# Attention and two MLPs in one kernel: five units of raw weight words under way, batch 1 loaded before unit 6, and the first w_out unit converted ahead of the softmax splits

## The chip, the cores and the metric

One core of one Trainium2 chip. The metric is the time of one launch in device microseconds, the median of several runs; lower is better. The engines are PE (TensorE, matmuls), DVE (VectorE), ACT (ScalarE), POOL (GpSimd) and SP (SyncE, which here issues nearly all the DMAs). Each works through its own queue in order and waits on semaphores of the others.

## The reference

All in float32. The attention has 8 batches, 8 heads, 576 rows of 64; `p` has 32 rows a head. `x` then has 4608 rows of 512, and each MLP has `w_in` of 512x2048 and `w_out` of 2048x512.

```python
p_packed = sm_attn(p, k, v)          # softmax(p k^T / 8) v
out = sm_attn(q, p_packed, p_packed)
x = out.transpose(0, 2, 1, 3).reshape(B * S, H * D)
h = x @ w_in1
x = (h * (1.0 / (1.0 + np.exp(-h)))) @ w_out1
h = x @ w_in2
out = (h * np.clip(h + 3.0, 0.0, 6.0) / 6.0) @ w_out2
```

## The kernel before

**Stages.** A prologue computes the attention of batch 0. Then come nine blocks of 512 tokens through MLP 1, and at the end MLP 2 over pairs of blocks. Block j runs sixteen hidden columns f of 128: hidden(f), called H0 to H15 here (line 860 on, 6 matmuls of 512 columns on PE for j = 0), then SiLU and the split of g into `gh` (ACT, line 889) and `gl` (DVE, line 890), and with a lag of two the projection of f - 2, called P0 to P15 (lines 897 to 899, 12 matmuls). In block 0 the attention of batch 1 stands between them: transposes of k and q (line 377), scores (line 417), softmax and the product with v.

**Splits.** Each factor of a float32 product is kept as a high part and a rest, and a product takes three matmuls: high by high, high by rest, rest by high. Hidden columns of block 0 multiply `fused` (w_in folded with the packed values, four groups g of four columns, made by `fuse`, lines 417, 611 and 617) with the weights of the softmax (`a2h`, `a2l`, lines 555 and 561).

**Raw words and units.** `w_in1` and `w_out1` arrive as raw 64-bit words and are turned into float32 on the chip. That goes in 16 units of 512 KB x 2: `in(g, c)` (two for each group g) and `out(k)` (the columns f = 2k and 2k + 1 of w_out), in the order in(0,0), in(0,1), out 0, in(1,0), in(1,1), out 1, out 2, in(2,0), in(2,1), out 3, out 4, in(3,0), in(3,1), out 5, out 6, out 7: units 0 to 15. A unit is loaded by `load_raw` on SP into a `raw` tile (`RAW = 3` of them), and converted by `conv_a` and `conv_b` (ACT, lines 148 and 154), `conv_shift` and `conv_sign` (DVE, lines 163 and 167) and `conv_add` (POOL, lines 177 and 179). A w_out unit then has `conv_hi` (two casts on ACT, line 192) and `conv_lo` (two subtractions on DVE, line 199), which give the weights of P(2k) (`wr`) and P(2k + 1) (`wo`); `keep` stores the odd ones in DRAM. `ct`, which conv_b writes, has two buffers, `cr` has four.

**Order.** Everything stands in the queues in the order in which the Python code runs; there is no scheduler behind it. `Feed.plan` puts each unit's steps at ticks: `STARTS` gives a unit's first tick, and the load of a later unit stands at its sixth. `LOADS` puts the loads of batch 1 (`load_p`, `load_tail`, `load_next`) at ticks too. In block 0, one tick is run for each 4.5 matmuls. Before block 0 the units 0 and 1 are written out by hand (`beginning`, `ending`), unit 2 and the rest go by ticks. `fill` runs matmuls on PE whose result is not used. In the prologue, part of the rows that the weights `wr` will take serve as `spare` room for q and v (`two_kb`).

Of the kernel before, what the change touches and what calls it, by code (L numbers as in the profile page):

```python
# [18 lines left out]
def tile_pack_attention_two_mlps(ctx: ExitStack, tc, q, k, v, p, w_in1, w_out1, w_in2, w_out2, out):  # L19
    nc = tc.nc  # L20
    B, H, S, D = q.shape
    NP = p.shape[2]
    NT, DM = out.shape
    DFF = w_in1.shape[1]
    P = 128
    T = 512
# [4 lines left out]
    NF = DFF // P  # L31
# [3 lines left out]
    RAW = 3  # L35
# [11 lines left out]
    wts = opened(first_left, "wts")  # L47
# [3 lines left out]
    cv = opened(first_block, "cv", side="right")  # L51
# [26 lines left out]
    early = [True]  # L78
    load_queue = [nc.sync]
    banks = [(ps_h, "h"), (ps_h, "h"), (ps_acc, "acc0"), (ps_acc, "acc1"), (ps_h, "h"), (ps_h, "h"), (ps_acc, "acc2")]  # L80
    spare = [(f, n) for f in range(0, NF, 2) for n in range(2)]
    shared = {}

    def bank():
# [10 lines left out]
    def two_kb():  # L95
        f, n = spare.pop()
        if f not in shared:
            shared[f] = wts.tile([P, 2, T], F32, tag=f"wr{f}", name="spare")
        return shared[f][:, n]


# [6 lines left out]
    made = {}  # L108
    raws = {}
    kept = []  # L110

    def half_w(f):
        if f % 2 == 0:
            return wts.tile([P, 2, DM], F32R, tag=f"wr{f}", name=f"wr{f}")
        return gp.tile([P, 2, DM], F32R, tag="wo", name="wo", bufs=WO)

    def load_raw(key):
        raw = cv.tile([P, 2, 2 * T], I32, tag="raw", name="raw", bufs=RAW)
        for i in range(2):
            if key[0] == "in":  # L120
                _, g, c = key
                src = w_in1.bitcast(I32)[(2 * c + i) * P:(2 * c + i + 1) * P, 2 * g * T:2 * (g + 1) * T]
            else:
                f = 2 * key[1] + i
                src = w_out1.bitcast(I32)[f * P:(f + 1) * P, :]
            nc.sync.dma_start(out=raw[:, i], in_=src)
        raws[key] = raw
# [399 lines left out]
    def sum2(lo, hi):  # L527
        g = (hi - lo) // NP
        st["s2", lo] = s = at.tile([P, (2 * S - T) // NP, 1], F32, tag="s2s", name="s2s", bufs=2)
        nc.vector.reduce_sum(out=s[:, 0:g, 0], in_=groups(lo, hi), axis=AX.X)  # L530

    def rec2(lo, hi):
        s = st["s2", lo][:, 0:(hi - lo) // NP]
        nc.vector.tensor_scalar_add(out=s, in0=s, scalar1=EPS)
        nc.vector.reciprocal(out=s, in_=s)

    def mul2(lo, hi, engine):
        g = (hi - lo) // NP
        engine.tensor_tensor(out=groups(lo, hi), in0=groups(lo, hi), in1=st.pop(("s2", lo))[:, 0:g].to_broadcast([P, g, NP]), op=ALU.mult)
# [801 lines left out]
    class Feed:  # L1341
# [6 lines left out]

        def load(self):
            if self.loaded < len(self.keys):  # L1350
                load_raw(self.keys[self.loaded])
                self.loaded += 1

        def plan(self):
            self.steps, self.ready = {}, set(self.keys[:2])
            for first, key in zip(STARTS, self.keys[2:]):
                todo = [(0, conv_a), (1, conv_b), (3, conv_shift), (4, conv_sign), (6, conv_add)]
                if key[0] == "out":
                    todo += [(9, conv_hi), (11, conv_lo)]
                todo += [(todo[-1][0], self.ready.add)]  # L1360
                for off, fn in todo:
                    self.steps.setdefault(first + off, []).append((off, lambda fn=fn, key=key: fn(key)))
                self.steps.setdefault(first + 6, []).append((20, lambda: self.load()))
                if key[0] == "out":
                    self.steps.setdefault(first + 15, []).append((21, keep))
            for first, fn in LOADS:
                self.steps.setdefault(first, []).append((30, fn))
            self.last = max(self.steps)
# [10 lines left out]
        def end(self):  # L1379
            while self.at <= self.last:  # L1380
                self.advance()

    FILL = (9, 10, 8, 20)
    STARTS = (-9, -6, -2, 1, 6, 9, 12, 15, 20, 24, 28, 31, 37, 42)
    LOADS = [(1, lambda: load_p(1)), (1, lambda: load_tail(1, "k"))]
    LOADS += [(2 + i, lambda i=i: load_next(i + 1)) for i in range(6)]
    LOADS += [(8, lambda: load_tail(1, "v")), (9, lambda: load_tail(1, "q"))]
    feed = Feed()
    feed.plan()
    feed.at = min(STARTS)  # L1390
# [21 lines left out]
        load_nat(0, "v", c)  # L1412
    load_tail(0, "v")
    load_tail(0, "q")
    feed.load()
    feed.load()
    feed.load()

    def beginning(key):
        conv_a(key)  # L1420
        conv_b(key)

    def ending(key):
# [73 lines left out]
    exp2(*SOFT2[1])  # L1497
    ending(unit[1])
    feed.load()
    fill(FILL[2])  # L1500
    to = fuse_products(0, 0)
    fill(FILL[3])
    turn_on(AF.Silu)
    feed.advance()
    feed.advance()
    made_ = fuse_high(0, 0, to)
    sum2(*SOFT2[0])
    rec2(*SOFT2[0])
    mul2(*SOFT2[0], nc.vector)
    sum2(*SOFT2[1])  # L1510
    rec2(*SOFT2[1])
    mul2(*SOFT2[1], nc.vector)
    turn_u(0, 0)
    high_u(0, 0, st["u", 0, 0])
    fuse_low(0, 0, to, made_)
    low_u(0, 0, st["u", 0, 0])
    turn_u(0, 1)
    high_u(0, 1, st["u", 0, 1])
    low_u(0, 1, st["u", 0, 1])
    while feed.at < 0:  # L1520
        feed.advance()
    early[0] = False
# [97 lines left out]
```

## Time and profile before

| | us |
|---|---|
| median of 3 runs (1492.5 to 1494.75) | 1492.56 |
| the profiled execution, its own time | 1489.72 |
| its span | 1487.9 |
| PE busy in the span | 1451.9 (98%) |
| DVE busy | 1008.4 (68%) |
| ACT busy | 725.0 (49%) |

All times below are of the profiled execution, counted from the start of its span; 1.82 us lie around the span. A row of a timeline has start, duration, engine, line, operation, output and inputs, and in brackets how long the engine had stood idle and which instruction released it. The duration of a matmul is modelled; what it costs is read from one start to the next.

### The profile page before, as it was taken

To read this page: it belongs to the slowest core of one execution; us is meant where nothing else is said; L and a number is where in the kernel's file an instruction comes from. 1 tells how busy PE (TensorE), PEld (TensorE's weight loads), DVE (VectorE), ACT (ScalarE), POOL (GpSimd) and SP (SyncE) were. 2 spreads that over 40 slices of the span, in tenths; PEclk is the share of its full clock that TensorE was granted. 3 is DMA by queue.
4 is the path that set the end of the run, shared out by engine and by line. 5 is a ranking of instruction groups with operands and counts; after the bars stand their busy time and mean duration, and the time that the engine had idled before them with its cause. 6 is when DMAs were issued, how large, how long until landed. Compare 5 with 4: busy or idle time off the path is not lost.

```text
span 1487.9 us, 21936 instructions
## 1 busy us (share of the span) xinstructions
PE 1451.9 (98%) x8002; PEld 1179.2 (79%) x8002; DVE 1008.4 (68%) x1555; ACT 725.0 (49%) x1107; POOL 179.9 (12%) x133
## 2 busy tenths in 40 slices
PE   7789999999999999999999999999999999999998
PEld 4557677777777676778888888888888889999998
DVE  5676555555656565645754769776977787878777
ACT  4584545555555555465553344343533443444443
POOL 1332111111112111132320000000000000000000
PEclk8899999999999999999999999999999999999999
DMA  7793686857585767489964676678667867998887
GB/s 239 199 290 91 202 243 172 205 164 169 159 205 155 200 153 209 121 224 250 279 195 155 193 245 199 190 227 262 203 194 226 243 210 213 293 309 252 273 272 227
DMA packets 391051, 316.58 MB, mean 213 GB/s; under 512 B 185120, under 2 KB 288032, under 8 KB 390432
## 3 DMA queue, kind: packets, MB, share of 16 engines
q1 hardware_dynamic: 389048, 314.72, 72.8%
q8 instruction: 64, 1.05, 0.3%
q10 hardware_dynamic: 1896, 0.46, 0.2%
q14 instruction: 43, 0.35, 0.1%
HBM read 257.43 MB, written 57.67 MB: 212 GB/s over the span
## 4 chain that ended last, share of the span: by engine, by line
PE 88%; ACT 4%; DVE 4%; DMA 2%; issue 1%; SPq 1%; POOL 0%; ACTq 0%; DVEq 0%; POOLq 0%
PE acc L897 8%; PE b L1161 8%; PE b L1163 8%; PE b L1162 8%; PE b L1256 8%; PE acc L898 8%; PE acc L899 8%; PE b L1258 8%; PE b L1259 8%; PE hps L870 4%; PE hps L872 4%; PE hps L871 4%; PE abank L417 3%; DMA nat<-in_v_dram 1%; PE abank L481 1%
## 5 line engine op out<-in xcount | busy, mean ns | idle before, releaser
L890 DVE TENSOR_TENSOR gl<-hps,gh 128x512 fp32r<-128x512 f32 x144 | 99.2, 689 | 200.1 <-ACT gh L889 199.9
L1161 PE MATMUL b<-xc,ws 128*128 128x512 f32 (+1 forms) x560 | 205.7, 367 | 0.7 <-ACT x L963 0.7
L1258 PE MATMUL b<-ro,ws 128*128 128x512 f32 (+2 forms) x564 | 206.2, 366 | 0.0
L1259 PE MATMUL b<-ro,ws 128*128 128x512 f32 (+2 forms) x564 | 206.2, 366 | 0.0
L1163 PE MATMUL b<-xc,ws 128*128 128x512 f32 (+1 forms) x560 | 205.6, 367 | 0.0
L1162 PE MATMUL b<-xc,ws 128*128 128x512 f32 (+1 forms) x560 | 205.6, 367 | 0.0
L1204 DVE TENSOR_TENSOR ro<-g,ro 128x1024 fp32r<-128x1024 f32 (+1 forms) x140 | 161.4, 1158 | 42.2 <-ACT ro L1199 41.8
L1199 ACT CAST ro<-g 128x1024 fp32r<-128x1024 f32 (+1 forms) x140 | 131.8, 965 | 94.0 <-DVE g L1192 34.6
L882 ACT ACTIVATE hps<-hps 128x512 f32<-128x512 f32 x144 | 84.0, 583 | 141.8 <-PE hps L872 141.4
L1256 PE MATMUL b<-ro,ws 128*128 128x512 f32 (+2 forms) x564 | 138.9, 367 | 0.3
L897 PE MATMUL acc<-gh,wr 128*128 128x512 f32 x288 | 117.2, 407 | 5.3 <-ACT gh L889 5.3
L1161 PEld LDWEIGHTS b<-xc,ws 128*128 128x128 f32 x560 | 105.1, 188 | 14.2 <-ACT x L963 1.1
L1259 PEld LDWEIGHTS b<-ro,ws 128*128 128x128 f32 x564 | 105.9, 188 | 13.1
L1258 PEld LDWEIGHTS b<-ro,ws 128*128 128x128 f32 x564 | 105.9, 188 | 13.1
L897 PE MATMUL acc<-gh,wo 128*128 128x512 f32 x288 | 114.3, 397 | 1.9 <-DMA wo<-w1o 1.9
L1162 PEld LDWEIGHTS b<-xc,ws 128*128 128x128 f32 x560 | 105.1, 188 | 13.2
L1163 PEld LDWEIGHTS b<-xc,ws 128*128 128x128 f32 x560 | 105.1, 188 | 13.1
L1256 PEld LDWEIGHTS b<-ro,ws 128*128 128x128 f32 x564 | 102.9, 188 | 15.0 <-DVE ro L1204 2.1
L898 PE MATMUL acc<-gl,wr 128*128 128x512 f32 x288 | 114.4, 397 | 0.2 <-DVE gl L890 0.2
L899 PE MATMUL acc<-gh,wr 128*128 128x512 f32 x288 | 113.9, 396 | 0.0
L899 PE MATMUL acc<-gh,wo 128*128 128x512 f32 x288 | 112.9, 392 | 0.0
L898 PE MATMUL acc<-gl,wo 128*128 128x512 f32 x288 | 112.9, 392 | 0.0
(176 smaller groups left out, 2636.0 us busy)
## 6 DMA issues: line engine op xcount, KB each, us to landing
ws<-w2in SPq DMA_DIRECT2D x280, 256.0 KB
ws<-w2out SPq DMA_DIRECT2D x280, 256.0 KB
wo<-w1o SPq DMA_DIRECT2D x64, 512.0 KB
x1d<-x SPq DMA_DIRECT2D x18, 512.0 KB
raw<-in_moe_w_in_dram SPq DMA_DIRECT2D x16, 512.0 KB
raw<-in_moe_w_out_dram SPq DMA_DIRECT2D x16, 512.0 KB
praw<-in_moe_w_in_dram SPq DMA_DIRECT2D x32, 256.0 KB
praw<-in_moe_w_out_dram SPq DMA_DIRECT2D x32, 256.0 KB
```

Of the source, the lines that this page charges most:

```text
L890: nc.vector.tensor_sub(out=gl, in0=g, in1=f32(gh))
L897: mm(acc[e], lhsT=w[:, 0, s], rhs=gh, start=first, stop=False)
L898: mm(acc[e], lhsT=w[:, 0, s], rhs=gl, start=False, stop=False)
L899: mm(acc[e], lhsT=w[:, 1, s], rhs=gh, start=False, stop=last)
L1161: mm(ps, lhsT=wh, rhs=xs[k][:, 0, c], start=first, stop=False, skip_group_check=True)
L1162: mm(ps, lhsT=wh, rhs=xs[k][:, 1, c], start=False, stop=False, skip_group_check=True)
L1163: mm(ps, lhsT=wl, rhs=xs[k][:, 0, c], start=False, stop=last, skip_group_check=True)
L1199: nc.scalar.copy(out=t[:, 0], in_=v)
L1204: nc.vector.tensor_sub(out=t[:, 1], in0=self.operand(s), in1=f32(t[:, 0]))
L1256: mm(to, lhsT=wh, rhs=x, start=False, stop=last, skip_group_check=True)
L1258: mm(to, lhsT=wh, rhs=x, start=first, stop=False, skip_group_check=True)
L1259: mm(to, lhsT=wl, rhs=x, start=False, stop=False, skip_group_check=True)
```

## The change

Five raw units are loaded at the start in place of three. The two more lie in rooms of the later weights `wr12` and `wr8` (`ROOM`), which `spare` tiles fill before; for that a `spare` tile and the weights of two even columns now share one tile of four parts (`pairs`). Units 8, 9 and 13 use those rooms again later. Batch 1's p, k and the first q are loaded in the prologue, between units 5 and 7, and no longer by ticks in block 0. Unit 2 (out 0) is written out by hand: its shift, sign and add stand ahead of the splits of the softmax weights, its casts before and after `low_u(0, 1)`. The sums, reciprocals and multiplications of the two softmax halves are paired. `STARTS` has one entry less, and from the fourth unit on its ticks are one to two earlier.

```diff
     def load_raw(key, room=None):
+        if room is None:
+            raw = cv.tile([P, 2, 2 * T], I32, tag="raw", name="raw", bufs=RAW)
+        else:
+            raw = wts.tile([P, 2, 2 * T], I32, tag=f"wr{room}", name="raw")
...
-            self.steps, self.ready = {}, set(self.keys[:2])
-            for first, key in zip(STARTS, self.keys[2:]):
+            self.steps, self.ready = {}, set(self.keys[:3])
+            for first, key in zip(STARTS, self.keys[3:]):
...
-                self.steps.setdefault(first + 6, []).append((20, lambda: self.load()))
+                if key != self.keys[9]:
+                    self.steps.setdefault(first + 6, []).append((20, lambda: self.load()))
...
+    ROOM = {3: 12, 4: 8, 8: 12, 9: 8, 13: 12}
-    STARTS = (-9, -6, -2, 1, 6, 9, 12, 15, 20, 24, 28, 31, 37, 42)
-    LOADS = [(1, lambda: load_p(1)), (1, lambda: load_tail(1, "k"))]
-    LOADS += [(2 + i, lambda i=i: load_next(i + 1)) for i in range(6)]
-    LOADS += [(8, lambda: load_tail(1, "v")), (9, lambda: load_tail(1, "q"))]
+    STARTS = (-6, -2, 1, 5, 8, 11, 14, 18, 22, 26, 29, 35, 40)
+    LOADS = [(6, keep), (8, lambda: load_tail(1, "v")), (9, lambda: load_tail(1, "q"))]
...
-    feed.load()
-    feed.load()
-    feed.load()
+    for _ in range(5):
+        feed.load()
...
     ending(unit[0])
     feed.load()
+    load_p(1)
+    load_tail(1, "k")
+    load_next(4)
...
     ending(unit[1])
     feed.load()
+    load_next(6)
...
-    feed.advance()
-    feed.advance()
+    beginning(unit[2])
     made_ = fuse_high(0, 0, to)
-    sum2(*SOFT2[0])
-    rec2(*SOFT2[0])
-    mul2(*SOFT2[0], nc.vector)
-    sum2(*SOFT2[1])
-    rec2(*SOFT2[1])
-    mul2(*SOFT2[1], nc.vector)
+    for i in range(2):
+        sum2(*SOFT2[i])
+    for i in range(2):
+        rec2(*SOFT2[i])
+    for i in range(2):
+        mul2(*SOFT2[i], nc.vector)
+    ending(unit[2])
+    feed.load()
...
     high_u(0, 1, st["u", 0, 1])
+    conv_hi(unit[2])
     low_u(0, 1, st["u", 0, 1])
+    conv_lo(unit[2])
```

On PE and on POOL no row moves. On ACT, from behind the last split of the prologue to the first SiLU of block 0, there stands before (`cr_467` is unit 2, `cr_502` and `cr_513` units 3 and 4, `cr_542` unit 5, `cr_609` unit 6, `hps_521` is H0, `kdg` the tail of batch 1's k):

```order
L148 ACTIVATE cr_502<-raw_408 128x1024
L154 ACTIVATE ct_505<-raw_408 128x1024
L148 ACTIVATE cr_513<-raw_424 128x1024
L154 ACTIVATE ct_515<-raw_424 128x1024
L192 CAST wr0_528<-cr_467 128x512
L192 CAST wo_530<-cr_467 128x512
L148 ACTIVATE cr_542<-raw_507 128x1024
L882 ACTIVATE hps_521<-hps_521 128x512
L889 CAST gh_545<-hps_521 128x512
```

and now (`cr_495` is unit 2, `cr_541`, `cr_547`, `cr_567` units 3, 4, 5):

```order
L201 CAST wr0_533<-cr_495 128x512
L201 CAST wo_535<-cr_495 128x512
L157 ACTIVATE cr_541<-raw_185 128x1024
L163 ACTIVATE ct_543<-raw_185 128x1024
L157 ACTIVATE cr_547<-raw_188 128x1024
L163 ACTIVATE ct_549<-raw_188 128x1024
L157 ACTIVATE cr_567<-raw_413 128x1024
L891 ACTIVATE hps_555<-hps_555 128x512
L898 CAST gh_570<-hps_555 128x512
```

The two casts of unit 2, before between units 4 and 5, now stand ahead of unit 3.

On DVE, from behind the sign step of unit 1 to the second split of the softmax weights, there stands before:

```order
L530 TENSOR_REDUCE s2s_477<-soft_100 128x16
L534 TENSOR_SCALAR s2s_477<-s2s_477 128x16
L535 RECIPROCAL s2s_477<-s2s_477 128x16
L539 TENSOR_TENSOR soft_100<-soft_100,s2s_477 128x512
L530 TENSOR_REDUCE s2s_482<-soft_100 128x20
L534 TENSOR_SCALAR s2s_482<-s2s_482 128x20
L535 RECIPROCAL s2s_482<-s2s_482 128x20
L539 TENSOR_TENSOR soft_100<-soft_100,s2s_482 128x640
L550 STREAM_TRANSPOSE abank_487<-soft_100 128x512
L617 TENSOR_TENSOR fused_472<-abank_435,fused_471 128x512
L617 TENSOR_TENSOR fused_475<-abank_436,fused_474 128x512
L561 TENSOR_TENSOR a2l_493<-abank_487,a2h_489 128x512
```

and now:

```order
L539 TENSOR_REDUCE s2s_505<-soft_100 128x16
L539 TENSOR_REDUCE s2s_507<-soft_100 128x20
L543 TENSOR_SCALAR s2s_505<-s2s_505 128x16
L544 RECIPROCAL s2s_505<-s2s_505 128x16
L543 TENSOR_SCALAR s2s_507<-s2s_507 128x20
L544 RECIPROCAL s2s_507<-s2s_507 128x20
L548 TENSOR_TENSOR soft_100<-soft_100,s2s_505 128x512
L548 TENSOR_TENSOR soft_100<-soft_100,s2s_507 128x640
L172 TENSOR_SCALAR cr_495<-cr_495 128x1024
L176 SCALAR_TENSOR_TENSOR cr_495<-raw_182,cr_495 128x1024
L559 STREAM_TRANSPOSE abank_521<-soft_100 128x512
L626 TENSOR_TENSOR fused_500<-abank_463,fused_499 128x512
```

The second sum has moved to the front, and the shift and the sign of unit 2 stand ahead of the first transpose (line 559). After that, DVE has before:

```order
L163 TENSOR_SCALAR cr_502<-cr_502 128x1024
L167 SCALAR_TENSOR_TENSOR cr_502<-raw_408,cr_502 128x1024
L163 TENSOR_SCALAR cr_513<-cr_513 128x1024
L890 TENSOR_TENSOR gl_546<-hps_521,gh_545 128x512
L199 TENSOR_TENSOR wr0_528<-cr_467,wr0_528 128x512
L199 TENSOR_TENSOR wo_530<-cr_467,wo_530 128x512
L167 SCALAR_TENSOR_TENSOR cr_513<-raw_424,cr_513 128x1024
L890 TENSOR_TENSOR gl_566<-hps_549,gh_565 128x512
L163 TENSOR_SCALAR cr_542<-cr_542 128x1024
```

and now:

```order
L208 TENSOR_TENSOR wr0_533<-cr_495,wr0_533 128x512
L208 TENSOR_TENSOR wo_535<-cr_495,wo_535 128x512
L172 TENSOR_SCALAR cr_541<-cr_541 128x1024
L176 SCALAR_TENSOR_TENSOR cr_541<-raw_185,cr_541 128x1024
L172 TENSOR_SCALAR cr_547<-cr_547 128x1024
L899 TENSOR_TENSOR gl_571<-hps_555,gh_570 128x512
L176 SCALAR_TENSOR_TENSOR cr_547<-raw_188,cr_547 128x1024
L899 TENSOR_TENSOR gl_586<-hps_574,gh_585 128x512
L172 TENSOR_SCALAR cr_567<-cr_567 128x1024
```

The two subtractions for `wr0` and `wo` no longer stand between `gl` of H0 and the sign step of unit 4.

On SP, from the first load of a raw unit on, there stands before:

```order
L126 DMA raw_177<-in_moe_w_in_dram 128x1024 x2
L126 DMA raw_180<-in_moe_w_in_dram 128x1024 x2
L126 DMA raw_183<-in_moe_w_out_dram 128x1024 x2
L126 DMA raw_408<-in_moe_w_in_dram 128x1024 x2
L126 DMA raw_424<-in_moe_w_in_dram 128x1024 x2
L126 DMA raw_507<-in_moe_w_out_dram 128x1024 x2
L126 DMA raw_525<-in_moe_w_out_dram 128x1024 x2
L324 DMA pn_536<-in_p_dram 128x1x64 x2
L330 DMA kt_539<-in_k_dram 64x8x64
L351 DMA nat_553<-in_k_dram 128x4x64 x2
L351 DMA nat_573<-in_k_dram 128x4x64 x2
L351 DMA nat_579<-in_k_dram 128x4x64 x2
```

and now:

```order
L135 DMA raw_176<-in_moe_w_in_dram 128x1024 x2
L135 DMA raw_179<-in_moe_w_in_dram 128x1024 x2
L135 DMA raw_182<-in_moe_w_out_dram 128x1024 x2
L135 DMA raw_185<-in_moe_w_in_dram 128x1024 x2
L135 DMA raw_188<-in_moe_w_in_dram 128x1024 x2
L135 DMA raw_413<-in_moe_w_out_dram 128x1024 x2
L333 DMA pn_416<-in_p_dram 128x1x64 x2
L339 DMA kt_419<-in_k_dram 64x8x64
L360 DMA nat_421<-in_k_dram 128x4x64 x2
L360 DMA nat_424<-in_k_dram 128x4x64 x2
L360 DMA nat_427<-in_k_dram 128x4x64 x2
L360 DMA nat_430<-in_k_dram 128x4x64 x2
```

Units 3 and 4 (`raw_185`, `raw_188`) now wait for the rooms of q and v, no longer for the raw tiles of units 0 and 1; unit 5 takes the tile of unit 0; and batch 1's p and k stand ahead of unit 6.

## Rows read from the trace of the kernel before

**Rows 1.** Busy time by stage; columns: stretch, length, PE, PEld, DVE, ACT, POOL, PEclk, DMA share, GB/s.
```profile
40.00:60.00 20.00, 14.95 (x70) 11.57 (x69) 16.55 (x19) 12.53 (x17) 8.45 (x4) 0.83 0.66 191
60.00:80.00 20.00, 16.63 (x79) 12.00 (x79) 10.04 (x16) 11.34 (x18) 7.01 (x4) 0.83 1.02 251
80.00:100.00 20.00, 16.51 (x100) 10.48 (x100) 18.02 (x25) 15.94 (x23) 8.10 (x5) 1.00 0.97 304
100.00:120.00 20.00, 17.68 (x151) 13.93 (x149) 9.66 (x17) 15.66 (x23) 6.93 (x3) 0.91 0.62 192
140.00:160.00 20.00, 19.48 (x111) 14.81 (x109) 15.72 (x26) 12.44 (x19) 1.04 (x1) 1.00 0.17 36
```

**Rows 2.** Timeline of PE: start, duration in us, instruction, idle before it and releaser.
```profile
51.33 0.79 PE L897 MATMUL acc<-gh,wr 128*128 128x512 f32 x1 [5.05 <-ACT gh L889]
...
53.25 0.63 PE L897 MATMUL acc<-gh,wr 128*128 128x512 f32 x1
...
53.68 0.63 PE L898 MATMUL acc<-gl,wr 128*128 128x512 f32 x1
...
66.65 0.79 PE L870 MATMUL hps<-a2h,fused 128*128 128x512 f32 x1 [3.37 <-ACT fused L611]
...
73.38 0.39 PE L899 MATMUL acc<-gh,wr 128*128 128x512 f32 x1
...
73.61 0.39 PE L870 MATMUL hps<-a2h,fused 128*128 128x512 f32 x1
...
83.73 1.09 PE L417 MATMUL abank<-T,pT 64*32 64x512 f32 x14 [1.87 <-ACT T L93]
...
95.59 0.50 PE L870 MATMUL hps<-a2h,fused 128*128 128x512 f32 x1 [0.71 <-ACT fused L611]
...
97.23 0.50 PE L872 MATMUL hps<-a2h,fused 128*128 128x512 f32 x1 [0.91 <-DVE fused L617]
...
110.29 0.63 PE L466 MATMUL abank<-ident,soft 128*64 128x128 f32 x2 [2.32 <-ACT T L93]
...
114.79 0.39 PE L870 MATMUL hps<-a2h,fused 128*128 128x512 f32 x1
...
164.38 0.47 PE L897 MATMUL acc<-gh,wo 128*128 128x512 f32 x1 [1.88 <-DMA wo<-w1o]
```

**Rows 3.** Timeline of ACT, same columns.
```profile
46.93 1.14 ACT L154 ACTIVATE ct<-raw 128x1024 int32<-128x1024 uint32 x1 [2.31 <-POOL cr L179]
...
50.70 0.58 ACT L889 CAST gh<-hps 128x512 fp32r<-128x512 f32 x1
...
59.78 0.37 ACT L93 COPY kdg<-abank 64x256 f32<-64x256 f32 x1 [4.17 <-DVE kdg L93]
...
66.02 1.07 ACT L611 CAST fused<-abank 128x512 fp32r<-128x512 f32 x2
...
73.82 1.12 ACT L148 ACTIVATE cr<-raw 128x1024 f32<-128x1024 f32 x1 [6.74 <-DMA raw<-in_moe_w_in_dram]
...
79.92 1.14 ACT L148 ACTIVATE cr<-raw 128x1024 f32<-128x1024 f32 x1 [1.81 <-DMA raw<-in_moe_w_out_dram]
```

**Rows 4.** Timeline of DVE and POOL, same columns.
```profile
32.79 1.91 DVE L534 TENSOR_SCALAR s2s<-s2s 128x16 f32<-128x16 f32 x1
...
42.11 0.68 DVE L163 TENSOR_SCALAR cr<-cr 128x1024 int32<-128x1024 int32 x1
...
53.12 1.22 DVE L167 SCALAR_TENSOR_TENSOR cr<-raw,cr 128x1024 int32<-128x1024 int32 x1
...
54.49 2.39 POOL L177 TENSOR_TENSOR wi<-cr,ct 128x1024 int32<-128x1024 int32 x1 [3.69 <-DVE cr L167]
...
54.86 2.57 DVE L163 TENSOR_SCALAR cr<-cr 128x1024 int32<-128x1024 int32 x1
```

**Rows 5.** Timeline of SP's queue, same columns.
```profile
27.18 5.85 SPq L126 DMA_DIRECT2D raw<-in_moe_w_in_dram  x4
...
70.87 7.90 SPq L126 DMA_DIRECT2D raw<-in_moe_w_out_dram  x4
```

More of the change, by code (lines that the diff above doesn't have):

```diff
@@ L80, in tile_pack_attention_two_mlps @@
     banks = [(ps_h, "h"), (ps_h, "h"), (ps_acc, "acc0"), (ps_acc, "acc1"), (ps_h, "h"), (ps_h, "h"), (ps_acc, "acc2")]
-    spare = [(f, n) for f in range(0, NF, 2) for n in range(2)]
+    PAIRED = NF // 2
+    spare = [(f, n) for f in range(PAIRED, NF, 4) for n in range(4)]
     shared = {}
@@ L97, in two_kb @@
         if f not in shared:
-            shared[f] = wts.tile([P, 2, T], F32, tag=f"wr{f}", name="spare")
+            shared[f] = wts.tile([P, 4, T], F32, tag=f"wr{f}", name="spare")
         return shared[f][:, n]
@@ L110, in tile_pack_attention_two_mlps, with load_raw @@
     kept = []
+    pairs = {}
     def half_w(f):
+        if f % 2 == 0 and f < PAIRED:
+            return wts.tile([P, 2, DM], F32R, tag=f"wr{f}", name=f"wr{f}")
         if f % 2 == 0:
-            return wts.tile([P, 2, DM], F32R, tag=f"wr{f}", name=f"wr{f}")
+            if f % 4 == 0:
+                pairs[f] = wts.tile([P, 2, 2, DM], F32R, tag=f"wr{f}", name=f"wr{f}")
+            return pairs[f // 4 * 4][:, f % 4 // 2]
         return gp.tile([P, 2, DM], F32R, tag="wo", name="wo", bufs=WO)
-    def load_raw(key):
-        raw = cv.tile([P, 2, 2 * T], I32, tag="raw", name="raw", bufs=RAW)
+    def load_raw(key, room=None):
+        if room is None:
+            raw = cv.tile([P, 2, 2 * T], I32, tag="raw", name="raw", bufs=RAW)
+        else:
+            raw = wts.tile([P, 2, 2 * T], I32, tag=f"wr{room}", name="raw")
         for i in range(2):
@@ L1350, in load @@
             if self.loaded < len(self.keys):
-                load_raw(self.keys[self.loaded])
+                load_raw(self.keys[self.loaded], ROOM.get(self.loaded))
                 self.loaded += 1
         def plan(self):
-            self.steps, self.ready = {}, set(self.keys[:2])
-            for first, key in zip(STARTS, self.keys[2:]):
+            self.steps, self.ready = {}, set(self.keys[:3])
+            for first, key in zip(STARTS, self.keys[3:]):
                 todo = [(0, conv_a), (1, conv_b), (3, conv_shift), (4, conv_sign), (6, conv_add)]
```

## The prediction

> **What bounds the kernel now.** PE is busy for 98% of the span, so time can only come from where it stands idle or runs slowly, and the change touches nothing behind block 0. The busy times by stage are read first: PE works 14.95, 16.63, 16.51 and 17.68 us of the four 20 us stretches from 40 to 120, 14.2 us short, and its granted clock averages 0.83, 0.83, 1.00 and 0.91 [rows 1]. Then PE's timeline: the gaps are 5.05 us ahead of P0, 3.37 ahead of H4, 1.87 ahead of batch 1's scores, 0.71 and 0.91 in H8, and 2.32 ahead of line 466, 14.23 in all [rows 2]. After the gaps of 5.05, 3.37 and 2.32 PE starts at half clock: two matmuls start 0.43 us apart at 53.25, and 0.23 at 73.38 [rows 2], which are the levels of 1.2 and 2.4 GHz. After 0.71, 0.91 and 1.87 the clock stays up. The releasers say who is late: ACT each time but one, which is DVE, so ACT's timeline comes third. It waits 2.31 us for POOL at 46.93, 4.17 for DVE at 59.78, and 6.74 and 1.81 for raw units to land at 73.82 and 79.92 [rows 3]. DVE and POOL come last, then SP: from 70.87 it needs 7.90 us to issue units 9 and 10 [rows 5].
>
> **The change part by part.** I follow the new order of each queue from 32 us on, with durations of before. On ACT a conversion pass takes 1.05 us from start to start, a cast or SiLU 0.5 to 0.6; on DVE a shift is 0.6 and a sign step 1.15 from start to start; an add on POOL is 2.4 [rows 3, 4].
>
> *A, the way to P0.* The scale step at 32.79 takes 1.91 us because it sits out POOL's add for unit 1 [rows 4]. The second sum, 0.8 us, now stands ahead of it, inside that wait: with its latency 0.95 saved. Shift and sign of unit 2 come in, 1.8 us. So the last split, which ends at 42.11 [rows 4], ends about 0.85 later; PE runs its unused matmuls until about 42 anyhow and loses nothing there, since it idles before P0. On ACT, from the last `a2h` cast (at 41.4 before, 42.25 now) to the end of H0's `gh` lie five passes, two casts, a SiLU and a cast, 7.5 us; before, the 2.31 us wait came on top, and `gh` started at 50.70 and ended at 51.28 [rows 3]. That wait was for unit 2's add. The add now starts behind the sign step at about 38.7 and is over at 41.1. So `gh` ends at 49.8, and P0 starts 1.5 us sooner. This gap is still some 3.5 us, P0 still starts at half clock, and I take nothing for it. **A: 1.45.**
>
> *B, the way to H4.* The sign step of unit 4 starts at 53.12, behind `gl` and two subtractions (1.2 us) for P0's weights; POOL's add follows at 54.49, and the shift at 54.86 sits it out and takes 2.57 us in place of 0.68 [rows 4]. With those subtractions done earlier the sign step starts at 50.45, the add at 51.7, and the shift ends at 54.65, 2.8 us sooner. Behind it the same five operations lead to the `kdg` copy on ACT, now 57.0 for 59.78. From there to the cast of `fused` at 66.02 [rows 3] were 6.24 us; one pass, 1.05, now stands ahead of `kdg`, inside ACT's wait. So the cast starts at 62.2 and H4 at 62.7 for 66.65. **A and B: 4.0.** PE would be there at 63.28 - 1.45 = 61.8, which leaves a gap of 0.9.
>
> *C, H4 and P2.* These 18 matmuls took 73.61 - 66.65 = 6.96 us [rows 2] for 18 x 0.23 = 4.14 at full clock. After a gap of 0.9 the clock should stay up, as after 0.71 and 0.91 before: 2.8 gained. But DVE now has the shift of unit 7 ahead of the subtractions for `wr2`, and it meets POOL's add of unit 6 (62.4 to 64.8, or a microsecond earlier); `wr2` is ready at 66.0 where P2's third matmul would start at 64.8: 1.3 lost, and 0.25 for the low half of `fused`. **C: 1.25**, from 2.3 to -1.55 if the clock falls anyway.
>
> *D, batch 1's scores.* The 1.87 us hang on a `T` copy of ACT behind a pass that waited 1.81 us for a unit in DRAM. Units 8 and 9 are now issued behind the sign steps of units 3 and 4, at about 47 and 52, and needed after 63; SP has nothing blocked ahead of them. The copy ends at 73, PE arrives at 75. **D: 1.87.** Units 3 and 4, issued from 27.18 on before [rows 5], now wait only for the rooms of q and v, which the prologue has read by then, and stand in the queue behind units 0 to 2, so they hold up neither; batch 1's p and k then fill SP until about 37, and unit 7 lands before 50, wanted at 57. I take nothing for these loads: the work that hides them is the softmax of batch 0 and the conversion of units 0 to 4. Without that cover they would cost what a late unit cost before, the 1.81 us at 79.92 [rows 3].
>
> *E, H8.* The gaps were 0.71 + 0.91. DVE has one sign step more ahead of the split of `fused`, and I come to 0.6 + 1.45. **E: -0.4**, from 0 to -1.5.
>
> *F, line 466.* It waited 2.32 us for an ACT copy; it now waits for DVE's `gl` of H9, which I put at 100.6, with PE arriving at 100.35. **F: 2.05**, at least 0.8 if ACT is a microsecond late.
>
> *G.* Line 466 and the 12 matmuls of P8, 114.79 - 110.29 = 4.5 us [rows 2], need 3.05 with no gap ahead. **G: 1.45**, or 0.
>
> Sum 1.45 + 2.55 + 1.25 + 1.87 - 0.4 + 2.05 + 1.45 = 10.2. The profiled execution took 1489.72 (span 1487.9), 2.84 below the median; it would take 1479.5. From the median of 1492.56: **1482.4 us**.
>
> **A rule against C and G.** The rows show half clock after gaps of 2.32 us and more, and none after 1.87 and less. The Trainium skill ("TensorE: Matmul & The Clock Gate", Part 1) says that the throttled state is the default, that activity releases it, and that the number of slow matmuls varies from run to run of one kernel. By that, a stretch of short waits like H4 to P2 may run slowly without one long gap. No run here shows it yet; the rival below has its price from rows.
>
> **The rivals.** *1. The clock stays low.* H4 to P2 and line 466 with P8 run slowly though their gaps are short. For it: PE stands still for some 2 us in H4 to P2 in pieces. Against: it did so in H8, 0.71 + 0.91, with no slow matmul. Price 2.8 + 1.45: gain 5.95, **1486.6**.
>
> *2. Nothing arrives at the end.* Block 1 opens with a 1.88 us wait for a load of `wo` at 164.38 [rows 2]. If that load came at a time of its own, what block 0 gains would be stood out there. Against: the DMA engines are busy for 0.17 of 140 to 160 [rows 1], so no backlog sets it, and the load is issued behind work of the same queues. That also covers a change that fails to pull the conversion ahead. Gain 0 to 3, **1491**.
>
> *3. Slower: ACT waits for POOL ahead of SiLU.* A `conv_b` needs a `ct` tile that POOL's add two units back sets free, and the SiLUs queue behind it. At 46.93 one such wait cost 2.31 us [rows 3]. With units further ahead in the queue than POOL, each of units 7 to 15 may pay it: nine times 2.31 is 20.8, against a gain of 10.2, **1503**. It decides from the fifth such wait on. Against: an add takes 2.4 us and I find the adds 6 us apart, with two waits of under 1.5 us, at units 8 and 9, where PE has slack.
>
> **How the numbers follow.** The forecast (gain 8 to 12) has 0.62, rival 1 0.2, rival 2 0.1, rival 3 0.05; 0.03 is left for a gain over 12. The range reaches from 1478.5 (14 us: all gaps and slow matmuls but A's) to 1489 (3.5: rival 1 with E and F at their lower ends), and holds the first two. 0.2% is 3 us, about what a measurement can tell from no change here. Faster: 0.62 + 0.2 + 0.03 and a little of rival 2, 0.86; the same 0.09; slower 0.05.
>
> **What would show it.** Right: P0 at about 49.8, with ACT in no wait for POOL ahead of it; the shift of unit 5 ending near 54.7; `kdg` near 57 and H4 near 62.7 after a gap of about 1 us at full clock; no ACT wait for a raw unit from 60 to 90; scores without a gap near 75; line 466 near 100.6. Wrong: matmuls 0.43 us apart behind 62; ACT rows waiting over 2 us for POOL; a gap of PE over 2 us anywhere from 60 to 115 (a step of the chain missed); or block 1's first wait much longer than 1.88.

## The result, and the profile after

The changed kernel takes **1480.21 us** (median; 1477.84 to 1482.2) against 1492.56 (1490.41 to 1494.75) for the kernel before, runs taken side by side: ratio 0.9917, 95% interval 0.9902 to 0.9931. The forecast was 1482.4, faster. The profiled execution took 1477.84 with a span of 1476.0, against 1489.72 and 1487.9. In the new file a helper's line has a number 9 higher.

Busy time by stage, the columns of [rows 1]:

```profile
40.00:60.00 20.00, 16.56 (x80) 12.68 (x79) 15.92 (x21) 16.20 (x23) 10.01 (x5) 0.91 0.90 284
60.00:80.00 20.00, 18.53 (x113) 12.12 (x112) 18.67 (x22) 16.30 (x23) 9.80 (x5) 1.00 1.02 307
80.00:100.00 20.00, 17.24 (x88) 12.90 (x87) 16.70 (x23) 16.34 (x24) 7.38 (x4) 0.91 0.71 206
100.00:120.00 20.00, 20.00 (x177) 14.60 (x176) 16.07 (x20) 12.81 (x21) 7.20 (x3) 1.00 0.43 83
```

PE's busy time rises in each stretch, and the last one is full. The low clock (0.91) stands in 80 to 100 now, where before it was 1.00.

PE's timeline, the rows that answer to [rows 2]:

```profile
49.78 0.49 PE L906 MATMUL acc<-gh,wr 128*128 128x512 f32 x1 [3.11 <-ACT gh L898]
...
51.78 0.63 PE L906 MATMUL acc<-gh,wr 128*128 128x512 f32 x1
52.21 0.63 PE L907 MATMUL acc<-gl,wr 128*128 128x512 f32 x1
...
62.91 0.50 PE L879 MATMUL hps<-a2h,fused 128*128 128x512 f32 x1 [1.31 <-ACT fused L620]
...
75.06 1.09 PE L426 MATMUL abank<-T,pT 64*32 64x512 f32 x16
...
76.44 0.50 PE L906 MATMUL acc<-gh,wr 128*128 128x512 f32 x1
...
89.44 0.80 PE L881 MATMUL hps<-a2h,fused 128*128 128x512 f32 x1 [2.03 <-DVE fused L626]
90.03 0.63 PE L879 MATMUL hps<-a2h,fused 128*128 128x512 f32 x1
90.46 0.63 PE L880 MATMUL hps<-a2l,fused 128*128 128x512 f32 x1
...
101.52 0.41 PE L475 MATMUL abank<-ident,soft 128*64 128x128 f32 x2
...
154.28 0.47 PE L906 MATMUL acc<-gh,wo 128*128 128x512 f32 x1 [1.96 <-DMA wo<-w1o]
154.59 0.40 PE L907 MATMUL acc<-gl,wo 128*128 128x512 f32 x1
154.82 0.40 PE L908 MATMUL acc<-gh,wo 128*128 128x512 f32 x1
```

H4's gap shrinks from 3.37 to 1.31 us. Batch 1's sixteen score matmuls stand in one row, and line 475 (466 before) shows no wait. One thing is worse: H8's third matmul waits 2.03 us for DVE, and the matmuls behind it start 0.43 us apart, which is 1.2 GHz.

ACT's `kdg` copy and the shift of unit 5 on DVE, for [rows 3] and [rows 4]:

```profile
57.02 0.37 ACT L94 COPY kdg<-abank 64x256 f32<-64x256 f32 x1 [1.70 <-DVE kdg L94]
...
62.26 1.08 ACT L620 CAST fused<-abank 128x512 fp32r<-128x512 f32 x2
```

```profile
50.37 1.22 DVE L176 SCALAR_TENSOR_TENSOR cr<-raw,cr 128x1024 int32<-128x1024 int32 x1
...
52.51 2.16 DVE L172 TENSOR_SCALAR cr<-cr 128x1024 int32<-128x1024 int32 x1
```

ACT waits for no raw unit from 40 to 120; its longest wait there for POOL is 1.26 us.

### The profile page after: what moved, and what is told of

Read it like the earlier page. It is cut to its first block, busy times and chain, and to the rows that moved or that the text cites. A ratio compares the mean times of both kernels' runs of the same rounds, so it can differ in the third digit from the quotient of the medians.

```text
span 1476.0 us, 21930 instructions
## 1 busy us (share of the span) xinstructions
PE 1447.3 (98%) x8002; PEld 1176.1 (80%) x8002; DVE 1013.0 (69%) x1555; ACT 725.6 (49%) x1107; POOL 179.9 (12%) x133
## 4 chain that ended last, share of the span: by engine, by line
PE 89%; DVE 4%; ACT 3%; DMA 2%; issue 1%; SPq 1%; POOL 0%; ACTq 0%; POOLq 0%; DVEq 0%
PE acc L906 8%; PE b L1170 8%; PE b L1171 8%; PE b L1172 8%; PE b L1265 8%; PE acc L907 8%; PE acc L908 8%; PE b L1268 8%; PE b L1267 8%; PE hps L879 5%; PE hps L881 4%; PE hps L880 4%; PE abank L426 3%; DVE cr L176 1%; PE abank L490 1%
```

## The experiments

For all kernels I read where PE's work starts, counted from the row of line 499 (508) near 20.8 us, since that row itself moves by up to 0.84 us from execution to execution. Times are medians; the runs of one kernel spread over 2 to 7 us, and the profiles show the clock falling at different waits. The kernel before was run again beside each group of experiments, with medians from 1490.73 to 1491.67, so times of different groups compare best by their ratios to it.

| kernel | us | P0 | H4 | P4 | H9 | 466/475 | H11 |
|---|---|---|---|---|---|---|---|
| before | 1492.56 | 30.56 | 45.88 | 64.33 | 80.25 | 89.52 | 94.02 |
| changed | 1480.21 | 28.71 | 41.84 | 55.37 | 73.67 | 80.45 | 83.44 |
| e1_order | 1489.07 | 28.71 | 44.22 | 62.93 | 78.42 | 87.72 | 92.29 |
| e2_loads | 1484.58 | 30.53 | 45.91 | 60.58 | 76.09 | 85.41 | 88.40 |
| e3_batch1_late | 1480.07 | 28.73 | 41.87 | 55.35 | 73.67 | 80.48 | 83.49 |
| e4_unit11_later | 1478.00 | 28.72 | 41.86 | 55.33 | 70.37 | 78.33 | 81.33 |
| e5_old_ticks | 1483.10 | 28.69 | 42.84 | 57.49 | 73.01 | 82.31 | 85.29 |
| e6_warm | 1477.48 | 28.83 | 41.88 | 56.43 | 72.19 | 79.62 | 82.64 |
| e7_late_casts | 1480.12 | 28.70 | 42.98 | 57.09 | 74.87 | 81.65 | 84.64 |
| e8_wo_early | 1475.29 | 28.71 | 42.26 | 55.73 | 70.80 | 78.74 | 81.73 |
| e9_both | 1476.17 | 28.73 | 42.31 | 55.82 | 70.86 | 78.48 | 81.46 |
| e10_three | 1482.68 | 29.19 | 43.27 | 56.76 | 75.10 | 82.04 | 85.02 |
| e11_after (changed, again) | 1479.57 | 28.71 | 41.86 | 55.36 | 72.12 | 79.59 | 82.57 |
| e12_three_late | 1487.73 | 28.71 | 45.71 | 61.19 | 80.92 | 87.72 | 90.72 |

### Order alone, loads alone, ticks alone

**Order alone** (the kernel before with unit 2 by hand and the paired softmax; old loads and ticks):

```diff
-    STARTS = (-9, -6, -2, 1, 6, 9, 12, 15, 20, 24, 28, 31, 37, 42)
+    STARTS = (-6, -2, 1, 6, 9, 12, 15, 20, 24, 28, 31, 37, 42)
...
+    beginning(unit[2])
...
+    ending(unit[2])
```

> The kernel before with the prologue's new order alone: unit 2 written out by hand as in the changed kernel, but three raw tiles, batch 1 loaded by ticks and the old ticks for units 3 on. Theory (A and B hang on the order, D on the loads): P0 starts near 49.8 in place of 51.33, H4 near 63 in place of 66.65, and ACT still waits for a raw unit of words ahead of unit 8 or 9, so batch 1's scores still stand behind a gap and most of the 4 us is given back there: 1487 to 1491. Rival 1 (the order makes nearly all of it): the gain of 10 to 12 us comes whole, 1480 to 1483, and no ACT wait for a raw unit over 1 us is left. Rival 2 (all of it is loads): P0 and H4 stand where they stood within 0.5 us and the time is that of before, 1492.5.

Measured 1489.07, ratio 0.9988 (0.9978 to 0.9997). P0 comes as early as in the changed kernel: term A belongs to the order. Also `kdg` comes at 56.91, where the changed kernel has it, but H4 only at 44.22, 2.4 us later than there (65.2 in the trace; I had expected 63). ACT stands idle for 1.31 us ahead of unit 7's first pass (the trace names a load of p as what ended it). And by the old ticks three conversion passes stand between `kdg` and the fused cast, where the changed kernel has two and the third ahead of `kdg`. PE still stalls at the scores. ACT and PE:

```profile
56.91 0.37 ACT L93 COPY kdg<-abank 64x256 f32<-64x256 f32 x1 [2.97 <-DVE kdg L93]
...
61.47 1.14 ACT L148 ACTIVATE cr<-raw 128x1024 f32<-128x1024 f32 x1 [1.31 <-DMA pn<-in_p_dram]
...
64.56 1.04 ACT L611 CAST fused<-abank 128x512 fp32r<-128x512 f32 x2
```

```profile
81.59 1.78 PE L417 MATMUL abank<-T,pT 64*32 64x512 f32 x14 [2.17 <-ACT T L93]
```

So B needs more than the order: the order frees the chain, and ACT must then neither wait for a load nor have the third pass behind `kdg`. The run without the new ticks (below) puts that pass at 1.0 us.

**Loads alone** (the changed kernel with the old order and old ticks):

```diff
-    STARTS = (-6, -2, 1, 5, 8, 11, 14, 18, 22, 26, 29, 35, 40)
+    STARTS = (-9, -6, -2, 1, 6, 9, 12, 15, 20, 24, 28, 31, 37, 42)
...
-    beginning(unit[2])
+    feed.advance()
+    feed.advance()
```

> The changed kernel with the prologue's old order and the old ticks: five raw units under way and batch 1 loaded early, and nothing else. Theory: P0 at 51.3 and H4 at 66.6 as before with the 5.05 and 3.37 us gaps, no ACT wait for a raw unit between 60 and 90, scores without a gap (2.9 us sooner), then line 466 (475 here) sooner by at most the same 2.9 plus its own gap: 1485 to 1489. Rival 1 (loads are hidden anyway, the order makes all of it): 1491 to 1493. Rival 2 (loads make all of it): 1480 to 1483.

Measured 1484.58, ratio 0.9961 (0.9948 to 0.9975), 0.4 under the theory's end. P0 and H4 stand where they stood, the scores have no gap, and ACT waits for no raw unit from 60 to 90:

```profile
80.03 1.09 PE L426 MATMUL abank<-T,pT 64*32 64x512 f32 x16
81.05 0.43 PE L439 MATMUL abank<-kdg,pT 128*32 128x128 f32 x8
81.41 0.50 PE L906 MATMUL acc<-gh,wr 128*128 128x512 f32 x1
```

From H5 to P4 it needs 8.57 us, as the changed kernel does; before, 11.49. The difference, 2.92, is term D measured by itself. Line 475 still waits 2.37 us here, as in order alone (2.35): neither part makes F.

**Ticks alone undone** (units 6 to 15; loads and order stay):

```diff
-    STARTS = (-6, -2, 1, 5, 8, 11, 14, 18, 22, 26, 29, 35, 40)
+    STARTS = (-6, -2, 1, 6, 9, 12, 15, 20, 24, 28, 31, 37, 42)
```

> The changed kernel with the old ticks for units 6 to 15 (each one to two later); loads and prologue order stay as changed. From the last prologue row on (PE's line 508 near 21 us), H4 stood at 41.84, H8 at 65.61, H9 at 73.67 and line 475 at 80.45 in the changed kernel. Theory (the ticks, and neither loads nor order, removed the wait ahead of line 475, and they made H8's): H4 at 41.8, H9 near 70.4 with no gap over 1 us in H8, then a gap of 2.4 us ahead of line 475 for an ACT copy, line 475 near 79.7 and P8 behind it slow or not: 1479 to 1481. Rival (loads and order removed the wait of line 475): line 475 near 77.2 without a gap, 1476 to 1477.5.

Measured 1483.1, ratio 0.9951 (0.9937 to 0.9964). H8 loses its long gap, and the wait ahead of line 475 is back: the ticks made both. In the profiled executions the two cancel: from P4 to line 475 it takes 25.19 us before, 25.08 in the changed kernel and 24.82 here. PE:

```profile
63.91 0.50 PE L879 MATMUL hps<-a2h,fused 128*128 128x512 f32 x1 [2.36 <-ACT fused L620]
...
65.45 0.63 PE L881 MATMUL hps<-a2h,fused 128*128 128x512 f32 x1
65.88 0.63 PE L906 MATMUL acc<-gh,wr 128*128 128x512 f32 x1
...
103.38 0.41 PE L475 MATMUL abank<-ident,soft 128*64 128x128 f32 x2 [2.36 <-ACT T L94]
...
103.86 0.40 PE L907 MATMUL acc<-gl,wr 128*128 128x512 f32 x1
104.09 0.39 PE L908 MATMUL acc<-gh,wr 128*128 128x512 f32 x1
```

The theory missed one thing: the ticks are also worth 1.0 us at H4, whose gap is 2.36 with them undone, and the clock fell behind it. P4 comes 2.1 us later by that, as much as the time is over what I expected.

### Which part of the loading counts

**Batch 1 late** (its loads by ticks again):

```diff
-    load_p(1)
-    load_tail(1, "k")
-    load_next(4)
...
+    LOADS += [(2 + i, lambda i=i: load_next(i + 1)) for i in range(6)]
```

> The changed kernel with batch 1's p, k and q loaded by ticks in block 0 again, as before; five raw units and the new order stay. Theory (batch 1's early load only clears SP's queue for units 8 to 10): H4 still near 62.9, units 8 and 9 issued later, and an ACT wait for a raw unit or for batch 1's k of at most 2 us ahead of the scores: 1480 to 1483. Rival (it is the early load of batch 1 that removes the scores' gap): the gap of about 1.9 us or more ahead of the scores is back, and with it 2.9 to 5 us: 1483 to 1486.

Measured 1480.07, ratio 0.9932 (0.9916 to 0.9949): every row of the table stands within 0.05 us of the changed kernel's. The rival fell: the scores have no gap, and undoing batch 1's early load alone costs nothing up to H11.

**Three raw units under way:**

```diff
-                if key != self.keys[9]:
+                if True:
...
-    ROOM = {3: 12, 4: 8, 8: 12, 9: 8, 13: 12}
+    ROOM = {}
...
-    for _ in range(5):
+    for _ in range(3):
```

> The changed kernel with three raw units under way as before; the prologue's order, batch 1's early loads and the new ticks stay. Theory (of the loads, the two further raw units are what counts, and batch 1's early load without them stands ahead of the raw units on SP): P0 as changed, ACT waits for a raw unit ahead of H4 or the scores by 1 to 7 us, the gaps at H4 and at the scores are back: 1487 to 1491. Rival (batch 1's early load clears SP for units 6 to 9): scores without a gap, 1480 to 1483.

Measured 1482.68, ratio 0.9948 (0.9932 to 0.9965); the changed kernel on the same chip (below) gave 1479.57. My theory fell: the scores have no gap, and H4 comes 1.4 us later behind a gap of 1.35, as short as the changed kernel's. ACT waits for a raw unit by 0.36 us ahead of P0, which comes 0.48 later, and by 0.97 ahead of H4. It also waits by 2.44, 1.06 and 1.64 behind H4 (at 66.92, 72.29 and 81.44), where PE's rows don't move: H5 to P4 takes 8.56 us.

**Both undone** (the edits of the two runs above):

> The changed kernel with both parts of the loading undone: three raw units under way, batch 1's p, k and q by ticks in block 0; the prologue's order and the new ticks stay. Each alone undone gave 1480.1 (batch 1 late) and 1482.7 (three units). Theory (either of the two clears SP for units 6 to 9, so their worths don't add): both gaps are back, H4 at 44 from the last prologue row in place of 41.84, ACT waits of 1 to 6 us for a raw unit, batch 1's scores behind a gap of about 2: 1485 to 1488. Rival (they add): 0 + 3 us, 1482 to 1484, H4 near 43.3 and scores without a gap.

Measured 1487.73, ratio 0.9968 (0.9954 to 0.9982). In the rows the two don't add: H4 comes 0.03 and 1.43 us later with one undone and 3.87 with both, and P4 by -0.02, 1.39 and 5.82. The times don't show it: beside the changed kernel's 0.9929 (below) the ratios make 0.4 and 2.8 us apart and 5.8 together, and the interval of each is 2 us or more to either side. H4, at 45.71, is later than the 44 I had expected and its gap the largest of all, and ACT's longest waits in 40 to 120 (view of waits: engine, line, releaser, total us, times, longest) are the raw units:

```profile
66.10 0.80 PE L879 MATMUL hps<-a2h,fused 128*128 128x512 f32 x1 [5.32 <-ACT fused L620]
```

```profile
ACT cr L157 <- DMA raw<-in_moe_w_in_dram: 9.2, 4, 4.5
```

Ahead of H4, ACT waits for raw units by nothing with batch 1 late, by 1.33 us with three units and by 3.97 with both undone: either part alone removes most of that wait. Whether it goes by the order of the loads on SP or by what the DMA engines have to share, these runs don't split. At the scores this kernel shows no gap, and yet its sixteen matmuls take 1.93 us in place of 1.09, and H5 to P4 9.45 in place of 8.57.

### H8, the clock, and the casts

**Unit 11 two ticks later:**

```diff
-    STARTS = (-6, -2, 1, 5, 8, 11, 14, 18, 22, 26, 29, 35, 40)
+    STARTS = (-6, -2, 1, 5, 8, 11, 14, 18, 24, 26, 29, 35, 40)
```

> The changed kernel with unit 11 started two ticks later (22 becomes 24), so that on DVE the split of fused for H8 stands ahead of the shift and the sign step of unit 11. Theory (the 2.03 us gap at H8's third matmul comes from the shift and sign ahead of the split, and the nine matmuls 0.43 us apart behind it from that gap): split near 87.1, the gap under 1 us, the clock full behind it, H9 about 2.5 to 3 us sooner, and the end too unless something absorbs it: 1477 to 1478. Rival 1 (the gap is given back at lines 471 and 475, where the softmax of batch 1 sets the time): H9 sooner, line 475 where it was, 1480. Rival 2 (unit 11's add now comes late for the last group of fused): a gap ahead of H12, 1481 to 1483.

In the changed kernel, POOL's add for unit 10 and behind it DVE ahead of H8; then DVE in this kernel:

```profile
82.89 2.40 POOL L188 TENSOR_TENSOR cr<-cr,ct 128x1024 int32<-128x1024 int32 x1 [2.69 <-DVE cr L176]
...
84.71 1.13 DVE L208 TENSOR_TENSOR wr<-cr,wr 128x512 fp32r<-128x512 f32 x1
...
86.37 0.68 DVE L172 TENSOR_SCALAR cr<-cr 128x1024 int32<-128x1024 int32 x1
86.97 0.68 DVE L94 COPY T<-abank 128x512 f32<-128x512 f32 x1
87.57 1.21 DVE L176 SCALAR_TENSOR_TENSOR cr<-raw,cr 128x1024 int32<-128x1024 int32 x1
88.71 1.28 DVE L626 TENSOR_TENSOR fused<-abank,fused 128x512 fp32r<-128x512 f32 x2
```

```profile
85.63 0.68 DVE L94 COPY T<-abank 128x512 f32<-128x512 f32 x1
86.23 1.27 DVE L626 TENSOR_TENSOR fused<-abank,fused 128x512 fp32r<-128x512 f32 x2
87.43 0.68 DVE L172 TENSOR_SCALAR cr<-cr 128x1024 int32<-128x1024 int32 x1
```

The gap at the third matmul falls from 2.03 to 0.31, no matmul is slow (in the changed kernel seven are, not nine), and H9 comes 3.3 us sooner, of which some 1.5 is the clock. Line 475 then waits 1.02 us for a `gl`, and H11 is 2.1 us sooner. In the second profile of the changed kernel (below), where the clock stays up in H8, H9 is 1.75 and H11 1.24 us behind this kernel's. Measured 1478.0, ratio 0.9919 (0.9906 to 0.9932): that the two steps of unit 11 make the gap is shown by the rows; 2 us of median alone are less than a measurement here can tell.

**Unused matmuls ahead of P0** (14 of them; what the kernel computes is the same):

```diff
-    WARM = {..., ("out", 0): 0, ...}
+    WARM = {..., ("out", 0): 14, ...}
```

> The changed kernel with 14 matmuls of 128 columns, whose result is not used, ahead of P0, in the 3.1 us in which PE stands idle. Theory (H4 is set by the kdg copy's chain on DVE, not by PE): P0 starts where it did, its matmuls go at full clock or not, its end comes up to 1 us sooner, and H4 stays at 41.8 from the last prologue row: 1480, no change. Rival (PE's slow clock in P0 is paid at the end): H4 a microsecond sooner and 1479. Third case (the matmuls run slowly and end late): P0 up to 0.5 later, H4 unmoved.

Measured 1477.48, ratio 0.9912 (0.9899 to 0.9925). P0 runs at full clock and ends 1.1 us sooner, and H4 stays at 41.88, as the theory said: its gap just grows to 2.82. Then the clock falls there instead:

```profile
62.24 0.50 PE L879 MATMUL hps<-a2h,fused 128*128 128x512 f32 x1 [2.82 <-ACT fused L620]
...
63.56 0.63 PE L879 MATMUL hps<-a2h,fused 128*128 128x512 f32 x1
63.98 0.63 PE L880 MATMUL hps<-a2l,fused 128*128 128x512 f32 x1
```

P4 comes 1.06 us later by it, and yet H11 0.8 sooner: with PE later at H8, DVE's split is late by 1.00 us in place of 2.03, and no matmul is slow there. Neither case had named this. The changed kernel's second profile has H11 at 82.57, where it stands here, and the ratios' intervals overlap, so that the time below 1479 is a gain of these matmuls is not shown.

**Casts of unit 2 late** (back at their old ticks):

```diff
-    conv_hi(unit[2])
...
-    conv_lo(unit[2])
...
+    LOADS = [(0, lambda: conv_hi(unit[2])), (2, lambda: conv_lo(unit[2])), (6, keep)]
```

> The changed kernel with the two casts and two subtractions of unit 2 at their old ticks (between units 4 and 5 on ACT, behind H0's gl on DVE); its shift, sign and add stay early. Theory (term B: the 1.2 us of subtractions push the sign step of unit 4 and with it POOL's add and the shift of unit 5, which sits the add out): the shift of unit 5 ends 1.2 to 2.8 us later, kdg and H4 with it (43.0 to 44.6 from the last prologue row in place of 41.84), and nothing behind gives it back: 1481.4 to 1483. Rival (the early add of unit 2 was all that B needed): H4 at 41.8 to 42.2 and 1480.

The shift of unit 5 ends 1.18 us later from the common row, H4 comes at 42.98, 1.14 us later, and the 1.2 us stand up to H11 (84.64 for 83.44). So the mechanism of B holds for the two subtractions. The median, 1480.12, ratio 0.9932 (0.9916 to 0.9948), doesn't show it, within a spread of 1477.5 to 1483.5. The early casts are worth 1.1 us at H4; whether any of it reaches the end stays open.

### A version that is faster than both

**Block 1's first `wo` load earlier**, on top of unit 11's two ticks:

```diff
-        while want_out and now >= NF - 2 and ...
+        while want_out and now >= NF - 4 and ...
```

> The kernel with unit 11 two ticks later (1478.0 before this run), and in it block 1's first load of wo issued two columns sooner, so that on SP it no longer stands behind a load of q that waits for a DVE copy for 21 us. Theory (the 1.9 us wait at block 1's first projection is that queue, so block 0's gain passes it whole and the load itself costs nothing): no gap there, the clock full behind it, 2 to 3.6 us less: 1474.5 to 1476. Rival 1 (the wait for v 20 us later takes it up): the gap gone, the next one longer by as much, 1478. Rival 2 (the DMA engines set it): the gap stays.

In the changed kernel, SP's waits from 115 to 165 have one of 21.3 us, a load of q behind a copy on DVE, and the `wo` loads stand in the queue behind it, at 147.65; in the new one the first stands ahead of it:

```profile
SPq L356 <- DVE T L393: 21.3, 1, 21.3
```

```profile
147.65 1.59 SPq L234 DMA_DIRECT2D wo<-w1o  x3
```

```profile
121.16 0.45 SPq L234 DMA_DIRECT2D wo<-w1o  x1
142.38 1.30 SPq L356 DMA_DIRECT2D nat<-in_q_dram  x2
```

Measured 1475.29, ratio 0.9895 (0.988 to 0.9911). The gap and the slow matmuls behind it are gone: the next hidden column starts at 132.08 from the common row, for 135.57 with unit 11's ticks alone. Of these 3.5 us the next wait, for v, takes 1.5 (that stretch, up to 153.77 for 155.74, is so much longer): rival 1 holds for this part, and 2.0 us stay.

**With unit 13 two ticks later as well** (29 becomes 31):

> The kernel of the earlier wo load (unit 11 two ticks later, block 1's first wo load two columns sooner) with unit 13 two ticks later too, so that on DVE the gl of H9 stands ahead of unit 13's shift, which sat out an add on POOL for 2.9 us. Theory: the 1.0 us gap ahead of line 475 shrinks to 0.5, 0.5 us less, no more than a measurement can tell: 1474.3 to 1475.5. Rival 1 (unit 13's later add delays the casts of its weights): a new gap in P10 to P12, 1476 to 1478. Rival 2 (gap goes and with it a slow stretch): 1473.

Measured 1476.17, ratio 0.9898 (0.9883 to 0.9913). Line 475's gap falls to 0.67, H11 gains 0.27, and the wait for v stands at 2.48: nothing gained. Beside this kernel and the one with three raw units, the changed kernel on the same chip:

> The changed kernel unchanged, beside the two others on one chip, so that its distance to them is measured in one place: 1480 plus or minus 1.5, some 5 above the kernel with both mends and 8 to 10 below the one with three raw units. If the clock behind the 1.9 us wait of block 1 varies from run to run, its runs spread over 3 us or more.

Measured 1479.57, ratio 0.9929 (0.9911 to 0.9946), runs from 1477.21 to 1482.95, while the version with all three edits (unit 11, `wo`, unit 13) ran from 1473.66 to 1477.27: the medians are 3.4 us apart, for some 5 expected. The kernel with three raw units is 3.1 slower, for 8 to 10 expected. The changed kernel's H8 has the same gap as the first profile, and no slow matmul behind it:

```profile
89.41 0.50 PE L881 MATMUL hps<-a2h,fused 128*128 128x512 f32 x1 [2.05 <-DVE fused L626]
89.74 0.40 PE L879 MATMUL hps<-a2h,fused 128*128 128x512 f32 x1
89.97 0.39 PE L880 MATMUL hps<-a2l,fused 128*128 128x512 f32 x1
```

## Why the prediction came out right

The mechanisms of A, B, D and F are in the rows. That the sum comes within 0.4 us is in part luck: C and D brought 1.8 us more than predicted, and E 2.0 less. By its own steps, counted from the row of line 499 (508):

| term | predicted | measured | where |
|---|---|---|---|
| A, P0 | 1.45 | 1.85 | 30.56 to 28.71 |
| B, H4 | 2.55 | 2.19 | A and B 4.04 for 4.0 |
| C, H4 and P2 | 1.25 | 2.00 | H4 to H5 6.96, now 4.96 |
| D, scores | 1.87 | 2.92 | H5 to P4 11.49, now 8.57 |
| E, H8 | -0.4 | -2.38 | P4 to H9 15.92, now 18.30 |
| F, line 466/475 | 2.05 | 2.49 | H9 to it 9.27, now 6.78 |
| G, P8 | 1.45 | 1.51 | it to H11 4.50, now 2.99 |
| sum | 10.2 | 10.58 | |

The profiled execution gained 11.9. Between 10.58 and that stand a start 0.3 later, and block 1: both kernels wait there about as long (1.88 and 1.96 us), but only before are the matmuls behind it slow, 1.6 us. Before, behind that wait:

```profile
165.08 0.63 PE L899 MATMUL acc<-gh,wo 128*128 128x512 f32 x1
165.51 0.63 PE L897 MATMUL acc<-gh,wo 128*128 128x512 f32 x1
```

I take this for chance and not for the change: of the kernels made from the changed one, two (`e4`, `e7`) are slow behind a wait of 2.09 and 1.99 us there, and the changed kernel's second profile, with 2.05, is not.

**A and B: right**, in size and in mechanism, and the unit 5 shift ended at 54.67 for 54.65. But B has conditions I gave no weight: it needs the raw units there sooner, and the new ticks. The prediction took nothing for the loads in A to C; alone, the order gains 1.66 at H4, not 4.0. Of the 2.4 that are missing, 1.3 is ACT's wait for a load and 1.0 the pass that the old ticks put behind `kdg`.

**C: right direction, too small.** The matmuls ran at full clock, as forecast, and the 1.3 us loss at `wr2` did not come. POOL's add of unit 6 was over at 64.16, and the shift of unit 7 started at 64.10: the add came early, and I had taken it to collide. The row now stands 0.16 us late.

**D: right mechanism, mis-sized.** ACT's `T` copy ended at 73.0 and PE came at 75.06, as I had put them. But I took the gap that the row shows, 1.87, for the stall. Two of the sixteen matmuls stand ahead of it in a row of 1.04 us whose end is modelled, and that row hid the rest:

```profile
80.82 1.04 PE L417 MATMUL abank<-T,pT 64*32 64x512 f32 x2
```

The next fourteen start at 83.73, 2.91 us later. From start to start the stall is 2.92, and the run with the loads alone gave the same. The Trainium skill ("Perfetto Trace Analysis", Tensor Engine Instruction) says that the end of a matmul in the trace is an estimate, and these rows agree.

**E: the term that failed.** The prediction had the gaps at 0.6 and 1.45; they were 0.73 and 2.03. The subtraction for `wr` at 84.71 took 1.13 in place of 0.68, beside an add on POOL from 82.89 to 85.3, and that I had not put in. The rest is the clock, 1.5 us (H8 to H9 took 8.06, and 6.52 in the repeated run). In that run P4 to H9 takes 16.76 and E is -0.84, inside its range of 0 to -1.5: what took it out of the range is the clock, which fell in one execution and not in the other. With this the mark "a gap over 2 us from 60 to 115" and "matmuls 0.43 apart behind 62" came true, at a place where I had looked and taken the smaller value. The runs also showed that E was no price of the loads or the order: unit 11's tick alone makes it.

**F and G: right in size, F partly by luck; the prediction did not say which part brings them.** The ticks do, not loads or order: with them undone the wait of 2.36 us is back, with either part alone it never went, and in the run with both loading parts undone it is gone. The size of F hangs on E: a PE that comes late from H8 has less to wait for at line 475. Where H8 has no slow matmul, H9 to line 475 takes 7.47 (the repeated run) and 7.96 (unit 11 later), so F is 1.80 and 1.31 there. In the latter a `gl` on DVE ends the wait, as I had put it.

**Rival 1** (clock low behind short waits) named the wrong place and the right kind: H4, P2 and P8 ran at full clock, H8 did not. The bound that I had read from the rows, half clock from 2.32 us on and full up to 1.87, does not hold: in the same trace of before the matmuls at 165.08 and 165.51 are slow behind 1.88, and line 475 without the new ticks runs at full clock behind 2.36. The Trainium skill's rule ("TensorE: Matmul & The Clock Gate", Part 1), that the number of slow matmuls varies from run to run, holds here: gaps of 2.03 and 2.05 at one place, slow behind one only. **Rival 2** (absorbed by block 1's `wo` load) fell: the wait moved with block 0, 1.88 to 1.96. **Rival 3** fell: from 40 to 120 ACT has no wait for POOL above 1.26.

## What to carry to other kernels

Read a stall from one start to the next, not from the bracket: a group of matmuls that is cut by a wait hides part of it. When a change has several parts, ask of each gain which parts it needs; here two parts of the loading could stand in for each other, so that undoing one moved H4 by at most 1.4 us and undoing both by 3.9. And when steps are moved on an engine that many wait for, list whose split or copy now stands behind them: here two ticks of one unit cost 1.8 to 3.3 us at the next hidden column.

## What the runs showed of the hardware

The clock does not follow the length of a gap alone. Gaps of 0.83 to 1.50 at H4 left it at full, and 2.36 to 5.32 there brought it to half. Over all places in 40 to 190 us of these profiles, gaps from 1.44 (H8 with the casts late) to 2.37 us (line 475 in loads alone) did either. At line 466 or 475, 2.32 and 2.35 brought it to half, and 2.36 and 2.37 left it at full. After the 3.11 us gap ahead of P0 in the changed kernel the matmuls still started 0.23 us apart up to 51.78, and only then six starts came at 0.43; with all three edits the same gap has them at 0.43 from the third on. And in these runs a slow stretch cost time only where PE was the one waited for: at P0 it cost nothing, at H4 1.06 us.
